# Rescheduling the first periods of a fused linear-attention and SwiGLU kernel, with q.kv in 64x64 tiles, one wide z broadcast and q transposed by DMA

## The chip, the cores and the metric

One Trainium2 chip (trn2), one core of it. The metric is the device time of one execution in microseconds, from runs without a profile, given as the median of several. The profile is one profiled execution; its span (first to last instruction) lies about 2 us below the run's time.

Engine names in the profile: PE is TensorE (matmuls), PEld its weight loads, DVE is VectorE, ACT is ScalarE, POOL is GpSimd, SP is SyncE (here it only issues DMAs).

## The reference, cut to what matters

```python
# q, k, v: 8 batches x 8 heads x 576 tokens x 64, float32
def _attn_ref(q, k, v):
    def phi(x): return np.where(x > 0, x, np.exp(x) - 1.0) + 1.0
    q_p, k_p = (phi(q), phi(k))
    kv = np.einsum('bhsd,bhse->bhde', k_p, v)        # one 64x64 matrix per head
    z = np.sum(k_p, axis=2)
    num = np.einsum('bhsd,bhde->bhse', q_p, kv)
    den = np.einsum('bhsd,bhd->bhs', q_p, z)[..., None] + 1e-06
    return (num / den)

def _moe_ref(x, w_gate, w_val, w_out):               # x: 4608 tokens x 512
    g = x @ w_gate                                   # 512 -> 1536
    silu = g * (1.0 / (1.0 + np.exp(-g)))
    return (silu * (x @ w_val)) @ w_out              # 1536 -> 512
```

## The kernel before

The network's 4608 tokens are done in nine *periods* of 512 tokens. A period g has twelve gate/value blocks (`l1`, eight 128x512 matmuls each) and four output blocks (`l2`, twelve matmuls each). A batch has nine slices j of 64 tokens, with one half of the heads (hh = 0) on partitions 0 to 63 and the other on 64 to 127; a period takes eight slices, so most periods take slices of two batches. While period g runs, the attention of batch g+1 is spread over its twelve `l1` slots and four `l2` slots, between the network's matmuls. In the traces each engine takes its calls in the order of the program (in run 7 below, ScalarE stands 7.33 us before one exp while a silu behind it has its input), so the slot of a call decides its place on each engine.

The attention steps that matter here:

```python
    def mm1(b, lp):              # kv and, in an extra column of ones, z
        if lp == 0:
            kvb[b] = (bank(), bank())
        W = 2 * D + 1
        for j in range(J):
            for hh in range(2):
                rows = slice(C * hh, C * hh + C)
                nc.tensor.matmul(
                    out=kvb[b][hh][:, 256 * lp:256 * lp + W], lhsT=kp[b % 2][rows, j, P * lp:P * lp + P],
                    rhs=vm[b % 2][rows, j, :, :].rearrange("p l c -> p (l c)")[:, 130 * lp:130 * lp + W],
                    start=(j == 0), stop=(j == J - 1))
    # zdiag (DVE): id16 * z column -> zd;  r_copies (ACT): kv blocks -> R
    def zb(b):                   # z broadcast over the partitions
        zps[b] = (bank(),) * 2
        for hh in range(2):
            nc.tensor.matmul(out=zps[b][hh][C * hh:C * hh + C, 0:HL * D], lhsT=ones[:, 0:C],
                             rhs=zd[:, 2 * hh:2 * hh + 2, :].rearrange("p i c -> p (i c)"), start=True, stop=True)
    # s3_prod, s3_reduce, s3_recip, s3_scale (DVE): q := q / (q.z), three groups of three slices (c = 0, 1, 2)
    def tr(b, c):                # transposes of q on TensorE, then tr_copy on ACT into qT
        ...
                nc.tensor.transpose(out=pt[:, 2 * jj + lp, :], in_=qp[b % 2][:, j0 + jj, P * lp:P * lp + P],
                                    identity=id16[:, :])
    def mm2(g, i, eng):          # q.kv -> xT[i], the network's input; R is block-diagonal 128x128
        ps = bank()
        ...
            nc.tensor.matmul(out=ps[:, c0:c0 + C * len(js)], lhsT=R[b % 2][:, i, :],
                             rhs=qT[b % 2][:, i, js[0]:js[-1] + 1, :].rearrange("p j c -> p (j c)"),
                             start=True, stop=True)
        # eviction to xT[i] by ACT or DVE
```

The schedules of before: `early` (periods 0 and 1: exp, phi, direct z sums `z_direct`, scaling and mm1 all inside the period before use; silu of four blocks by tanh, so that it shares a table with exp: in the trace no table load, 1.28 us each, stands between them), `late` (period 2) and `steady` (periods 3 to 6). The start of the program and the loads:

```python
    load(k, k16, 0, 0, 2)
    ...
    ld_v(0)
    ld_w1(0)
    ld_k(1)
    ld_w1(1)
    ld_w1(2)
    ld_q(1)
    ...
    def steady(b):
        sl[0] = [lambda: phi_q(b, 0), lambda: mm1(b, 0)]
        sl[1] = [lambda: phi_q(b, 1), lambda: mm1(b, 1)]
        sl[2] = [lambda: zdiag(b, 0), lambda: zdiag(b, 1), lambda: r_copies(b)]
        sl[3] = [lambda: zb(b), lambda: zb_copy(b), lambda: s3_prod(b, 0)]
        ...
        w = [
            [lambda: s3_scale(b, 2)],
            [lambda: tr(b, 2), lambda: tr_copy(b, 2, A)],
            [lambda: mm2(b, 0, V), lambda: mm2(b, 1, A)],
            [lambda: mm2(b, 2, V), lambda: mm2(b, 3, A)],
        ]
```

Of the kernel before, what the change touches and what calls it, by code (L numbers as in the profile page):

```python
# [17 lines left out]
def kernel(  # L18
# [47 lines left out]
    R = two([P, 4, P], FP16, "R")  # L66
    qT = two([P, 4, J, C], FP16, "qT")
# [20 lines left out]
    def chan(i):  # L88
        return 2 * (i % 2) + i // 2
# [30 lines left out]
    def phi(src, e, dst, b, lp):  # L120
        s = slice(2 * lp, 2 * lp + 2)
        nc.vector.tensor_scalar(out=e[:, s, :], in0=e[:, s, :], scalar1=1.0, scalar2=None, op0=ALU.min)
        for l in range(2 * lp, 2 * lp + 2):
            nc.vector.scalar_tensor_tensor(  # L124
                out=dst[b % 2][:, :, D * l:D * l + D],
                in0=src[b % 2][:, l, :].rearrange("p (j d) -> p j d", d=D), scalar=0.0,
                in1=e[:, l, :].rearrange("p (j d) -> p j d", d=D), op0=ALU.max, op1=ALU.add)
# [14 lines left out]
    def vcast(b, lp):  # L142
        s = slice(2 * lp, 2 * lp + 2)
        nc.scalar.activation(out=vm[b % 2][:, :, s, 0:D].rearrange("p j l d -> p l j d"),
                             in_=v16[b % 2][:, s, :].rearrange("p l (j d) -> p l j d", d=D),
                             func=AF.Copy, bias=0.0, scale=1.0)
# [4 lines left out]
    def mm1(b, lp):  # L151
        if lp == 0:
            kvb[b] = (bank(), bank())
        W = 2 * D + 1
        for j in range(J):
            for hh in range(2):
                rows = slice(C * hh, C * hh + C)
                nc.tensor.matmul(
                    out=kvb[b][hh][:, 256 * lp:256 * lp + W], lhsT=kp[b % 2][rows, j, P * lp:P * lp + P],
                    rhs=vm[b % 2][rows, j, :, :].rearrange("p l c -> p (l c)")[:, 130 * lp:130 * lp + W],  # L160
                    start=(j == 0), stop=(j == J - 1))
# [7 lines left out]
    def r_copies(b):  # L169
        for hh in range(2):  # L170
            kvv = kvb[b][hh][:, :].rearrange("p (i c) -> p i c", i=2)
            for h2 in range(2):
                rows, c = slice(D * h2, D * h2 + D), (D + 1) * h2
                nc.scalar.activation(
                    out=R[b % 2][rows, :, D * h2:D * h2 + D].rearrange("p (l a) c -> p a l c", a=2)[:, hh, :, :],
# [5 lines left out]
    def zb(b):  # L181
        zps[b] = (bank(),) * 2
        for hh in range(2):
            nc.tensor.matmul(out=zps[b][hh][C * hh:C * hh + C, 0:HL * D], lhsT=ones[:, 0:C],
                             rhs=zd[:, 2 * hh:2 * hh + 2, :].rearrange("p i c -> p (i c)"), start=True, stop=True)

    def zb_copy(b):
        nc.scalar.activation(out=zbc[:, :], in_=zps[b][0][:, 0:HL * D], func=AF.Copy, bias=0.0, scale=1.0)
# [43 lines left out]
    def tr(b, c):  # L232
        j0, j1 = js_of(c)
        tps[(b, c)] = bank()
# [6 lines left out]
    def tr_copy(b, c, eng):  # L241
        j0, j1 = js_of(c)
        src = tps[(b, c)][:, :].bitcast(FP16)[:, 0:2 * P * (j1 - j0)].rearrange("p (j i c) -> p j i c", j=j1 - j0, i=4)
        dst = qT[b % 2][:, :, j0:j1, :].rearrange("p i j c -> p j i c")
# [9 lines left out]
    def mm2(g, i, eng):  # L254
        ps = bank()
        us = units(g)
        for b in sorted(set(u[0] for u in us)):
            js = [j for (bb, j) in us if bb == b]
            c0 = C * us.index((b, js[0]))
            nc.tensor.matmul(out=ps[:, c0:c0 + C * len(js)], lhsT=R[b % 2][:, i, :],  # L260
                             rhs=qT[b % 2][:, i, js[0]:js[-1] + 1, :].rearrange("p j c -> p (j c)"),
                             start=True, stop=True)
        dst = xT[i][g % 2][:, :]
        if eng == "A":
            nc.scalar.activation(out=dst, in_=ps[:, :], func=AF.Copy, bias=0.0, scale=1.0 / SC)
        else:
            nc.vector.tensor_scalar(out=dst, in0=ps[:, :], scalar1=1.0 / SC, scalar2=None, op0=ALU.mult)  # L267


    def l1(g, fb, tanh=False):  # L270
        pg, pv = pG[fb % 2], pV[fb % 3]
        for (w, ps) in ((wg, pg), (wv, pv)):
            for i in range(4):
                nc.tensor.matmul(out=ps[:, :], lhsT=w[:, chan(i), P * fb:P * fb + P], rhs=xT[i][g % 2][:, :],  # L274
# [34 lines left out]

    load(k, k16, 0, 0, 2)  # L310
    load(k, k16, 0, 2, HL)
    load(q, q16, 0, 0, 2)
    nc.gpsimd.iota(out=idx[:, :], pattern=[[-1, P]], base=0, channel_multiplier=1)
# [3 lines left out]
    ld_k(1)  # L317
    ld_w1(1)
    ld_w1(2)
    ld_q(1)  # L320
# [5 lines left out]
    nc.vector.memset(ones[:, :], 1.0)  # L326
    nc.vector.memset(sil[0][:, :], 0.0)
    for i in range(2):
        nc.vector.memset(vm[i][:, :, :, D:D + 1], 1.0)
        nc.vector.memset(R[i][:, :, :], 0.0)  # L330

    A, V = "A", "V"

# [5 lines left out]
    def s3_all(b, c):  # L339
        s3_prod(b, c)  # L340
        s3_reduce(b, c)
        s3_recip(b, c)
        s3_scale(b, c)

# [3 lines left out]
    nc.vector.tensor_scalar(out=id16[:, :], in0=idx[:, :], scalar1=0.0, scalar2=None, op0=ALU.is_equal)  # L348
# [4 lines left out]
    for lp in range(2):  # L353
        vcast(0, lp)
        mm1(0, lp)
    r_copies(0)
    for c in ((0, 3), (3, 6), (6, 8)):
        s3_all(0, c)
        if c[0] == 6:
            warm(6)  # L360
        tr(0, c)
        tr_copy(0, c, A)
    warm(2)
    for i in range(4):
        mm2(0, i, A if i % 2 else V)
    warm(2)

    def s3a(b, c):
        return [lambda: s3_prod(b, c), lambda: s3_reduce(b, c)]

    def early(b):

        sl = [[] for _ in range(FB)]
        sl[0] = [lambda: exp_k(b, 0)]
        if b == 1:
            c8 = (8, 9)
            sl[5] = [lambda: s3_all(0, c8), lambda: tr(0, c8), lambda: tr_copy(0, c8, A)]
        sl[1] = [lambda: exp_k(b, 1)]
        sl[2] = [lambda: exp_q(b, 0)]
        sl[3] = [lambda: exp_q(b, 1)]  # L380
        sl[4] = [lambda: phi_k(b, 0)]
        sl[6] = [lambda: phi_k(b, 1)]
        sl[7] = [lambda: z_direct(b)]
        sl[8] = [lambda: phi_q(b, 0)]
        sl[10] = [lambda: phi_q(b, 1)]
        sl[11] = s3a(b, 0)
        w = [
            [lambda: s3_recip(b, 0), lambda: s3_scale(b, 0)] + s3a(b, 1)
            + [lambda: s3_recip(b, 1), lambda: tr(b, 0), lambda: tr_copy(b, 0, A)],
            [lambda: vcast(b, 0), lambda: vcast(b, 1), lambda: s3_scale(b, 1)] + s3a(b, 2)  # L390
            + [lambda: tr(b, 1), lambda: tr_copy(b, 1, A), lambda: s3_recip(b, 2), lambda: s3_scale(b, 2)],
            [lambda: mm1(b, 0), lambda: mm1(b, 1), lambda: r_copies(b), lambda: tr(b, 2), lambda: tr_copy(b, 2, A)],
            [lambda i=i: mm2(b, i, A if i % 2 else V) for i in range(4)],
        ]
        return sl, w

    def steady(b):

        sl = [[] for _ in range(FB)]
        sl[0] = [lambda: phi_q(b, 0), lambda: mm1(b, 0)]  # L400
        sl[1] = [lambda: phi_q(b, 1), lambda: mm1(b, 1)]
        sl[2] = [lambda: zdiag(b, 0), lambda: zdiag(b, 1), lambda: r_copies(b)]
        sl[3] = [lambda: zb(b), lambda: zb_copy(b), lambda: s3_prod(b, 0)]
        sl[4] = [lambda: s3_reduce(b, 0)]
        sl[5] = [lambda: s3_recip(b, 0), lambda: s3_prod(b, 1)]
        sl[6] = [lambda: s3_scale(b, 0)]
        sl[7] = [lambda: s3_reduce(b, 1), lambda: tr(b, 0), lambda: tr_copy(b, 0, A)]
        sl[8] = [lambda: s3_recip(b, 1), lambda: s3_prod(b, 2)]
        sl[9] = [lambda: s3_scale(b, 1)]
        sl[10] = [lambda: s3_reduce(b, 2), lambda: tr(b, 1), lambda: tr_copy(b, 1, A)]  # L410
        sl[11] = [lambda: s3_recip(b, 2)]
        w = [
            [lambda: s3_scale(b, 2)],
            [lambda: tr(b, 2), lambda: tr_copy(b, 2, A)],
            [lambda: mm2(b, 0, V), lambda: mm2(b, 1, A)],
            [lambda: mm2(b, 2, V), lambda: mm2(b, 3, A)],
        ]
        return sl, w

    def late(b):  # L420

        sl = [[] for _ in range(FB)]
        sl[0] = [lambda: phi_k(b, 0)]
        sl[1] = [lambda: phi_k(b, 1), lambda: mm1(b, 0)]
        sl[2] = [lambda: phi_q(b, 0), lambda: mm1(b, 1)]
        sl[3] = [lambda: zdiag(b, 0), lambda: zdiag(b, 1), lambda: r_copies(b)]
        sl[4] = [lambda: phi_q(b, 1), lambda: zb(b), lambda: zb_copy(b)]
        sl[5] = [lambda: s3_prod(b, 0)]
        sl[6] = [lambda: s3_reduce(b, 0)]
        sl[7] = [lambda: s3_recip(b, 0), lambda: s3_prod(b, 1)]  # L430
        sl[8] = [lambda: s3_scale(b, 0)]
        sl[9] = [lambda: s3_reduce(b, 1), lambda: tr(b, 0), lambda: tr_copy(b, 0, A)]
        sl[10] = [lambda: s3_recip(b, 1), lambda: s3_prod(b, 2)]
        sl[11] = [lambda: s3_scale(b, 1)]
        w = [
            [lambda: s3_reduce(b, 2), lambda: s3_recip(b, 2), lambda: tr(b, 1), lambda: tr_copy(b, 1, A)],
            [lambda: s3_scale(b, 2)],
            [lambda: tr(b, 2), lambda: tr_copy(b, 2, A), lambda: mm2(b, 0, V)],
            [lambda: mm2(b, 1, V), lambda: mm2(b, 2, A), lambda: mm2(b, 3, V)],
        ]  # L440
        return sl, w

# [70 lines left out]
```

## Time and profile before

368.75 us, median of 3 runs (368.16 to 369.24). From the page of the profile:

```profile
span 366.4 us, 4976 instructions
...
PE 326.5 (89%) x1866; PEld 153.9 (42%) x1866; DVE 231.4 (63%) x408; ACT 180.8 (49%) x266; POOL 39.3 (11%) x66
```

TensorE is the engine to look at. A busy share of 89% says little by itself: 1296 network matmuls start 0.2158 us apart when nothing hinders them, 31.08 us a period (144 x 0.2158), 279.7 us in nine. So I cut the span at the first gate matmul of each period. In the view by stretches (`--windows`), each line is a stretch (from:to), its length, then for PE, PEld, DVE, ACT and POOL the busy time and number of instructions, the granted TensorE clock, the DMA share and GB/s:

```profile
...
27.60:76.18 48.58, 37.85 (x228) 17.75 (x227) 29.75 (x52) 20.77 (x32) 8.55 (x14) 0.96 0.97 163
76.18:118.86 42.68, 38.05 (x225) 18.20 (x224) 29.17 (x49) 29.30 (x39) 3.65 (x6) 0.96 0.35 59
...
227.09:262.70 35.61, 35.41 (x211) 16.45 (x210) 26.52 (x48) 21.56 (x31) 0.00 (x0) 1.00 0.13 31
...
```

These are periods 0 and 1 and one of the four steady periods (3 to 6, all 35.6). Period 0 lasts 17.5 us longer than its matmuls, period 1 11.6, a steady one 4.5. What TensorE waited for, in all (line, matmul output, what it waited for, total us, times, longest):

```profile
...
PE pX_112 L238 <- DVE qp_73 L226: 7.6, 3, 5.0
PE pX_114 L238 <- DVE qp_73 L226: 2.4, 2, 1.9
PE pG_108 L274 <- DVE sil_97 L279: 2.3, 1, 2.3
```

(Left out above them: the wait for the first load, in the start.) The 5.0 us is in period 0: the transposes of the ninth slice wait for VectorE, which waited for ScalarE, which waited for the load of batch 1's q (ScalarE's timeline; the bracket is the idle time before, and what ended it):

```profile
36.24 1.16 ACT L118 ACTIVATE eq<-q_1_66 128x1152 f16<-128x1152 f16 x1 [3.52 <-DMA q_1_66<-in_q_dram]
```

Waits of that kind are most of the early periods' loss; matmuls at half rate after them are another part (six start 0.43 us apart from 45.8 to 47.9 us, right after the 5.0 us). In a steady period there is nearly none; there the 4.5 us is attention work on TensorE. Part of one, from the timeline (start, length with the pipeline's drain, line, output<-inputs, count):

```profile
220.70 0.50 PE L238 MATMUL pX_112<-id_105,qp_74 128*128 128x128 f16 x6
221.03 2.75 PE L293 MATMUL pV_110<-wo,hT_94 128*128 128x512 f16 x12
223.62 0.30 PE L260 MATMUL pX_113<-qT_84,R_82 128*128 128x320 f16 x1
...
224.06 2.75 PE L293 MATMUL pG_108<-wo,hT_94 128*128 128x512 f16 x12
227.31 0.38 PE L274 MATMUL pG_107<-xT_1_89,wg 128*128 128x512 f16 x1
227.89 0.38 PE L274 MATMUL pG_107<-xT_1_91,wg 128*128 128x512 f16 x1 [0.20 <-DVE xT_1_91 L267]
```

Lengths overlap, so read the distance between starts: a transpose block takes 221.03 - 220.70 = 0.33 us, mm2 two times 0.44, and the third gate matmul comes 0.58 instead of 0.22 us after the second, as xT (the network's input) is not yet there.

### The profile page before, as it was taken

Reading aid. Unit: us, or ns where it says so; the run is one execution under the profiler, and the core shown is the slowest. Engines: PE = TensorE matmul, PEld = TensorE weight load, DVE = VectorE, ACT = ScalarE, POOL = GpSimd, SP = SyncE. Lnnn points to the kernel's source line nnn. Section 1 sums busy time; section 2 is a strip of 40 time slices with the busy share of each in tenths; the row PEclk is TensorE's granted clock in tenths of the full one; section 3 lists DMA queues with packets and bytes.
Section 4 is the critical chain, followed back from the end, with each engine's and each line's share of the span. In section 5 each row is a group of like instructions: output and inputs, shape, how many; then the busy total and the mean of one; then the engine's idle time right before and its main releaser. Section 6 shows DMA issues by size and latency. Waiting matters only on the chain.

```text
span 366.4 us, 4976 instructions
## 1 busy us (share of the span) xinstructions
PE 326.5 (89%) x1866; PEld 153.9 (42%) x1866; DVE 231.4 (63%) x408; ACT 180.8 (49%) x266; POOL 39.3 (11%) x66
## 2 busy tenths in 40 slices
PE   0469288999879899999999999999999999999995
PEld 0334043543435344544454444444444444444442
DVE  2974639747595788787767885788488533323331
ACT  3645531576576348545854585459544234402310
POOL 8532211100111120111011000000000000000000
PEclk9999989999899999999999999999999999999999
DMA  7999994830446257348054703100300130022013
GB/s 107 196 206 207 207 187 64 144 90 2 64 64 126 58 73 121 71 110 131 0 87 98 126 2 86 29 2 18 82 18 2 29 87 2 0 57 59 0 29 86
DMA packets 23656, 28.63 MB, mean 78 GB/s; under 512 B 2128, under 2 KB 19024, under 8 KB 23632
## 3 DMA queue, kind: packets, MB, share of 16 engines
q0 software_dynamic: 17872, 18.88, 33.0%
q1 hardware_dynamic: 5760, 9.44, 10.3%
q8 instruction: 14, 0.23, 0.3%
q14 instruction: 10, 0.08, 0.1%
HBM read 37.75 MB, written 9.44 MB: 129 GB/s over the span
## 4 chain that ended last, share of the span: by engine, by line
PE 70%; DVE 12%; DMA 7%; issue 5%; ACT 3%; POOL 2%; DVEq 0%; POOLq 0%; ACTq 0%
PE pG_107 L274 11%; PE pG_108 L274 9%; PE pV_109 L274 7%; PE pV_111 L274 7%; PE pV_110 L274 6%; PE pG_108 L293 6%; PE pV_110 L293 6%; PE pG_107 L293 5%; PE pV_109 L293 5%; DMA q_1_66<-in_q_dram 4%; DMA wv<-in_moe_w_val_dram 3%; DVE hT_94 L283 2%; DVE den L213 1%; PE pX_112 L238 1%; DVE qp_74 L124 1%
## 5 line engine op out<-in xcount | busy, mean ns | idle before, releaser
L274 PEld LDWEIGHTS <-wv 128*128 128x128 f16 x432 | 42.5, 98 | 52.5 <-issue 2.6
L274 PEld LDWEIGHTS <-wg 128*128 128x128 f16 x432 | 40.6, 98 | 51.3 <-issue 8.1
L282 ACT ACTIVATE sil_96<-pG_107 128x512 f16<-128x512 f32 x50 | 29.9, 597 | 38.8 <-PE pG_107 L274 36.5
L282 ACT ACTIVATE sil_97<-pG_108 128x512 f16<-128x512 f32 x50 | 29.8, 597 | 36.3 <-PE pG_108 L274 33.0
L293 PEld LDWEIGHTS <-hT_94 128*128 128x128 f16 x240 | 23.2, 98 | 26.3
L293 PEld LDWEIGHTS <-hT_95 128*128 128x128 f16 x192 | 18.6, 98 | 21.1
L213 DVE TENSOR_REDUCE den<-prod 128x12 f32<-128x768 f16 (+2 forms) x25 | 22.9, 915 | 0.3
L195 PE MATMUL pX_113<-kp_71,ones 64*64 64x256 f16 x18 | 4.0, 402 | 11.6 <-DVE kp_71 L124 11.6
L293 PE MATMUL pV_110<-wo,hT_94 128*128 128x512 f16 x60 | 13.8, 379 | 0.0
L293 PE MATMUL pG_108<-wo,hT_94 128*128 128x512 f16 x60 | 13.8, 379 | 0.0
L293 PE MATMUL pV_109<-wo,hT_94 128*128 128x512 f16 x60 | 13.8, 379 | 0.0
L293 PE MATMUL pG_107<-wo,hT_94 128*128 128x512 f16 x60 | 13.8, 379 | 0.0
L283 DVE SCALAR_TENSOR_TENSOR hT_94<-pV_109,sil_96 128x512 f16<-128x512 f32 x10 | 6.9, 691 | 10.6 <-PE pV_109 L274 5.8
L274 PE MATMUL pG_108<-xT_0_86,wg 128*128 128x512 f16 x30 | 11.4, 380 | 2.3 <-DVE sil_97 L279 2.3
L274 PE MATMUL pG_107<-xT_0_90,wg 128*128 128x512 f16 x30 | 11.6, 387 | 0.4 <-DVE xT_0_90 L267 0.4
L226 DVE TENSOR_TENSOR qp_73<-qp_73,rden 128x768 f16<-128x768 f16 (+2 forms) x13 | 11.6, 892 | 0.3
L274 PE MATMUL pG_107<-xT_0_86,wg 128*128 128x512 f16 x30 | 11.7, 390 | 0.0
L274 PE MATMUL pG_107<-xT_0_92,wg 128*128 128x512 f16 x30 | 11.6, 387 | 0.0
L274 PE MATMUL pG_107<-xT_0_88,wg 128*128 128x512 f16 x30 | 11.6, 387 | 0.0
L118 ACT ACT_TABLE_LOAD x7 | 9.0, 1283 | 5.3 <-DMA k_0_63<-in_k_dram 5.2
L124 DVE SCALAR_TENSOR_TENSOR kp_72<-k_1_64,ek 128x576 f16<-128x576 f16 x16 | 11.4, 755 | 0.3
L124 DVE SCALAR_TENSOR_TENSOR kp_71<-k_0_63,ek 128x576 f16<-128x576 f16 x16 | 11.4, 755 | 0.3
(188 smaller groups left out, 751.9 us busy)
## 6 DMA issues: line engine op xcount, KB each, us to landing
out_dram<-osb_98 SPq DMA_DIRECT2D x24, 128.0 KB, 2.4
out_dram<-osb_99 SPq DMA_DIRECT2D x24, 128.0 KB, 2.4
out_dram<-osb_100 SPq DMA_DIRECT2D x24, 128.0 KB, 2.4
v_0_67<-in_v_dram POOLq DMA_DIRECT2D x8, 288.0 KB, 6.7
k_1_64<-in_k_dram POOLq DMA_DIRECT2D x8, 288.0 KB, 5.2
q_1_66<-in_q_dram POOLq DMA_DIRECT2D x8, 288.0 KB, 5.0
v_1_68<-in_v_dram POOLq DMA_DIRECT2D x8, 288.0 KB, 6.6
k_0_63<-in_k_dram POOLq DMA_DIRECT2D x6, 288.0 KB, 4.8
```

The lines of the kernel that those rows point to most:

```text
L118: nc.scalar.activation(out=e[:, s, :], in_=src[b % 2][:, s, :], func=AF.Exp, bias=0.0, scale=1.0)
L124: nc.vector.scalar_tensor_tensor(out=dst[b % 2][:, :, D * l:D * l + D], in0=src[b % 2][:, l, :].rearrange("p (j d) -> p j d", d=D), scalar ...
L195: nc.tensor.matmul(out=zps[b][hh][rows, 0:HL * D], lhsT=ones[rows, 0:C], rhs=kp[b % 2][rows, j, :], start=(j == 0), stop=(j == J - 1))
L213: nc.vector.tensor_reduce(out=den[:, HL * j0:HL * j1], in_=prod[:, 0:j1 - j0, :].rearrange("p j (l d) -> p (j l) d", d=D), axis=AX.X, op=A ...
L226: nc.vector.tensor_tensor(out=qv, in0=qv, in1=rden[:, HL * j0:HL * j1].unsqueeze(2).to_broadcast([P, HL * (j1 - j0), D]), op=ALU.mult)
L238: nc.tensor.transpose(out=pt[:, 2 * jj + lp, :], in_=qp[b % 2][:, j0 + jj, P * lp:P * lp + P], identity=id16[:, :])
L274: nc.tensor.matmul(out=ps[:, :], lhsT=w[:, chan(i), P * fb:P * fb + P], rhs=xT[i][g % 2][:, :], start=(i == 0), stop=(i == 3))
L282: nc.scalar.activation(out=s[:, :], in_=pg[:, :], func=AF.Silu, bias=0.0, scale=1.0)
L283: nc.vector.scalar_tensor_tensor(out=hT[g % 2][:, fb, :], in0=pv[:, :], scalar=SC * (0.5 if tanh else 1.0), in1=s[:, :], op0=ALU.mult, op1 ...
L293: nc.tensor.matmul(out=ps[:, :], lhsT=hT[g % 2][:, fb, P * t:P * t + P], rhs=wo[:, fb, :], start=(fb == 0), stop=(fb == FB - 1))
```

## The change

Its intent: take attention work off TensorE in the steady periods, and reorder the first two so that fewer engines wait. (a) mm2 becomes one pass of 64x64 tiles, four at a time, over the kv blocks themselves instead of block-diagonal 128x128 matrices, half of which are zeros, and moves ahead of the last output block (from period 1 on), so that its evictions are hidden. The heads are reordered for that. (b) z is broadcast by one full matmul of 512 columns. (c) mm1 is one block. (d) From batch 3 on q is transposed by DMA. (e) Loads, exps and the schedules of the first periods move: batch 1's q loads ahead of the second and third weight blocks, the loads of later batches and the exps of batches 1 and 2 come earlier, tanh stays in two blocks of period 0 only, and period 1 takes the `late` form, period 2 the steady one.

The diff, cut to its core:

```diff
-    R = two([P, 4, P], FP16, "R")
-    qT = two([P, 4, J, C], FP16, "qT")
+    R = two([P, 4, D], FP16, "R")
+    qT = two([P, J, 2, P], FP16, "qT")
 ...
-        zps[b] = (bank(),) * 2
+        zps[b] = bank()
+        nc.tensor.matmul(out=zps[b][:, :], lhsT=ones[:, :], rhs=zd[:, :, :].rearrange("p i c -> p (i c)"),
+                         start=True, stop=True)
 ...
     def tr(b, c):
         j0, j1 = js_of(c)
+        if b > 2:
+            nc.sync.dma_start_transpose(out=qT[b % 2][:, j0:j1, :, :].rearrange("p j l t -> p (j l) t"),
+                                        in_=qp[b % 2][:, j0:j1, :].rearrange("p j c -> p (j c)"))
+            return
 ...
+    def mm2(g, spare, engs):
+        ps = [bank(), bank(), bank(), spare]
+        ...
+                for lp in range(2):
+                    for e in range(2):
+                        rows = slice(D * e, D * e + D)
+                        nc.tensor.matmul(out=ps[2 * hh + e][D * lp:D * lp + D, c0:c0 + C * len(js)],
+                                         lhsT=R[b % 2][rows, 2 * lp + hh, :],
+                                         rhs=qT[b % 2][rows, js[0]:js[-1] + 1, lp, C * hh:C * hh + C],
+                                         start=True, stop=True)
 ...
     ld_k(1)
+    ld_q(1)
     ld_w1(1)
     ld_w1(2)
-    ld_q(1)
 ...
+        if c[0] == 3:                      # in the start-up
+            exp_k(1, 0)
+            exp_k(1, 1)
 ...
+    def first():                           # period 0; (slot, call)
+            (0, lambda: exp_q(1, 0)), (1, lambda: exp_q(1, 1)),
+            (2, lambda: phi_k(1, 0)), (4, lambda: phi_k(1, 1)), (5, lambda: z_direct(1)),
+            (6, lambda: phi_q(1, 0)), (7, lambda: phi_q(1, 1)),
+            (8, lambda: s3_a(0, c8)), (9, lambda: s3_b(0, c8)), (10, lambda: t_(0, c8)),
+            (10, lambda: s3_a(1, 0)), (11, lambda: s3_b(1, 0))])
+        ...                                # output blocks
+            (0, lambda: vcast(1, 0)), (0, lambda: vcast(1, 1)), (0, lambda: s3_a(1, 1)), (0, lambda: s3_b(1, 1)),
+            (1, lambda: t_(1, 0)), (1, lambda: s3_a(1, 2)), (1, lambda: exp_k(2, 0)), (1, lambda: exp_k(2, 1)),
+            (2, lambda: t_(1, 1)), (2, lambda: mm1(1)), (2, lambda: r_copies(1)), (2, lambda: s3_b(1, 2)),
+            (2, lambda: exp_q(2, 0)), (2, lambda: exp_q(2, 1)),
+            (3, lambda: t_(1, 2))])
 ...
-            l1(g, fb, tanh=(g < 2 and fb < NT))
+            l1(g, fb, tanh=(g == 0 and fb < 2))
 ...
         for t in range(4):
+            if t == 3 and b1 < NG and g > 0:
+                mm2(b1, pV[2], "AVAV")
             l2(g, t)
```

## The prediction

> **What bounds it now.** TensorE. In the timeline, back-to-back 128x512 matmuls start every 0.2158 us, so one period of the gated network (144 matmuls) costs 31.08 us, nine of them 279.7 of the 366.4 us span. The stretches between the periods' first gate matmuls: start-up 27.6, period 0 48.6, period 1 42.7, period 2 37.2, periods 3 to 6 35.4 to 35.6, period 7 32.5, period 8 31.1, tail 4.5 us. Granted clock 0.96 to 1.00. Start-up is 8% of the span; periods 0 and 1 exceed pure matmul time by 29 us, another 8%.
>
> Period 0's excess is mostly waits (list of waits): 5.0 us for the scaled ninth q slice, 2.3 us for a tanh fix behind a late q load, 1.9 and 1.0 for scale and phi. Period 1: 2.0, 1.9, 1.5.
>
> **A steady period's 4.5 us of attention on TensorE (timeline):** three transpose blocks 3 x 0.33; mm1 in two blocks 2 x 0.71, about 0.2 of each for changing the array's tiling (the Trainium skill, "TensorEngine Tiling (Array Packing)", Key Properties, says a mode change drains the array; the trace's longer spacing around the block agrees); z broadcast 0.49; mm2 0.88 plus 0.2 to 0.4 waiting for xT.
>
> **The change there.** DMA transposes take 1.0 off TensorE. One mm1 block saves 0.2. One z matmul of 512 columns saves 0.27. Four 64x64 tiles: estimate 2 x 0.22 + 0.2 for 0.88, and the xT evictions hide under the last output block: 0.5 together. The trace shows 64x64 tiles concurrent only in pairs (256 columns every 0.107 us); the same page, Available Configurations, lists four independent ones, which no run here shows. Sum about 2.1: 33.4 us. I stepped VectorE through it (26.5 us of work): it keeps up, zdiag just in time for the z matmul.
>
> The transposes' latency is off the path: a slice is scaled 6 us or more before the mm2 that reads it, the third a period before.
>
> **Early periods.** Period 0: q of batch 1 loads before the later weight blocks, exp of k moves ahead, tanh shrinks from four blocks to two. VectorE stays nearly full (about 31 us). Stepped through: waits of 2 us at z, 1.4 at the ninth slice, then at the end a serial chain (ScalarE's exp and copies, transpose, copy, mm2, xT) with 4 us of idle TensorE: 42.3 us. Period 1 takes period 2's form minus the savings: 36.2. Period 2 becomes steady: 33.5. Start-up: the exp table load (1.28 us) moves off, but loads bind again and exp of k1 delays the last q copy: gain 0.3. Period 7: gain 0.7.
>
> **Sum of gains, all on the TensorE path:** 0.3 + 6.3 + 6.5 + 3.7 + 4 x 2.1 + 0.7 = 26: span 340.5; runs lie about 2 us above it: 342.5 us. Range 337 to 349. Faster by over 2%: 0.97; within 2%: 0.02; slower: 0.01.
>
> **What would show each step.** Steady periods of 33.2 to 33.7 us; mm2 under 0.7 us; one mm1 block of 1.2 us; period 0 between 39 and 44 us with its largest TensorE wait at its end; period 1 about 36; first gate matmul near 27.3 us.
>
> **What would make it wrong.** (1) mm2's tiles do not overlap, or weight loads bind: up to 1.2 us a period, 9 in all. (2) DMA transposes slower than 6 us: TensorE waits before mm2 in periods 2 and 3. (3) VectorE's lag in early periods: plus or minus 4 us. (4) TensorE at half clock after waits (spacing 0.43 us, as at 45.8 us before): 1 to 3 us. (5) Reordered loads delay weight blocks past their use.

## The result, and the profile after

341.06 us, median of 4 runs (339.46 to 341.98), against 368.46 us for before (4 runs); ratio 0.926, 95% interval 0.921 to 0.931. Ratios here are the mean time of one kernel's fast runs over that of the other's fast runs of the same rounds, so not quite the ratio of the medians quoted. The prediction was 342.5 us, 337 to 349.

The page after:

```profile
span 340.2 us, 4865 instructions
...
PE 310.7 (91%) x1814; PEld 145.3 (43%) x1814; DVE 228.5 (67%) x405; ACT 170.1 (50%) x256; POOL 39.1 (11%) x66
```

The stretches after, cut the same way (periods 0 and 1 and one steady period):

```profile
...
27.19:69.85 42.66, 37.47 (x234) 17.94 (x234) 28.74 (x51) 24.15 (x36) 7.93 (x13) 0.96 1.10 194
69.85:106.01 36.16, 34.71 (x216) 16.45 (x216) 30.28 (x55) 25.65 (x36) 4.90 (x8) 1.00 0.42 71
...
205.97:239.30 33.33, 33.33 (x199) 15.33 (x198) 26.58 (x48) 19.48 (x29) 0.00 (x0) 1.00 0.28 54
...
```

In the steady period TensorE now counts as busy for all of its 33.33 us (a matmul's length includes its drain, so gaps of 0.1 us, like the one before the z broadcast below, do not show). All stretches, with what was predicted for each:

| stretch | before, us | predicted gain | measured after, us | measured gain |
|---|---|---|---|---|
| start | 27.60 | 0.3 | 27.19 | 0.4 |
| period 0 | 48.58 | 6.3 | 42.66 | 5.9 |
| period 1 | 42.68 | 6.5 | 36.16 | 6.5 |
| period 2 | 37.01 | 3.7 | 33.32 | 3.7 |
| periods 3 to 6, each | 35.61 | 2.1 | 33.32 | 2.3 |
| period 7 | 32.31 | 0.7 | 31.74 | 0.6 |
| period 8 and tail | 35.79 | 0 | 35.84 | -0.05 |

The gain of the start is not resolved: in the runs below that leave its order alone it ends between 26.5 and 27.7 us.

The waits of TensorE after:

```profile
...
PE pX_113 L273 <- ACT qT_85 L254: 2.5, 1, 2.5
...
PE pX_114 L197 <- DVE kp_72 L124: 1.5, 1, 1.5
PE pX_112 L183 <- DVE zd L165: 0.9, 1, 0.9
```

The waits of 5.0 and 2.3 us are gone. The three longest of what is left lie in periods 0 and 1 (those left out here are in the start): 2.5 us at the end of period 0 (mm2 waits for ScalarE's copy of the transposed q), 1.5 us at the direct z sums in period 0, 0.9 us at the z broadcast in period 1.

And a steady period's mm2, where the timeline of before showed its own:

```profile
202.81 0.32 PE L273 MATMUL pX_113<-qT_84,R_82 64*64 64x320 f16 x1
...
202.82 0.32 PE L273 MATMUL pX_114<-qT_84,R_82 64*64 64x320 f16 x1
202.97 0.24 PE L273 MATMUL pX_113<-qT_85,R_83 64*64 64x192 f16 x1
...
203.37 2.76 PE L308 MATMUL pG_108<-wo,hT_94 128*128 128x512 f16 x12
```

Four tiles (one is left out) start within 0.01 us, the next four 0.16 us later (320 columns). The whole pass, from where the next output matmul would have started (200.13 + 12 x 0.2158 = 202.72) to 203.37, takes 0.65 us against 0.88, and the gate matmuls wait for nothing. The Trainium skill, "TensorEngine Tiling (Array Packing)", Available Configurations, lists 64x64 as four tiles; the trace agrees: all four run at once.

### The profile page after: what moved, and what is told of

Its sections match the earlier page's. It is cut to its first block, busy times and chain, and to the rows that moved or that the text cites. A ratio compares the mean times of both kernels' runs of the same rounds, so it can differ in the third digit from the quotient of the medians.

```text
span 340.2 us, 4865 instructions
## 1 busy us (share of the span) xinstructions
PE 310.7 (91%) x1814; PEld 145.3 (43%) x1814; DVE 228.5 (67%) x405; ACT 170.1 (50%) x256; POOL 39.1 (11%) x66
## 4 chain that ended last, share of the span: by engine, by line
PE 75%; DMA 14%; ACT 3%; DVE 3%; issue 2%; POOL 2%; POOLq 0%; DVEq 0%
PE pG_108 L289 12%; PE pG_107 L289 12%; PE pV_111 L289 8%; PE pV_110 L289 8%; PE pV_109 L289 8%; DMA q_1_66<-in_q_dram 7%; PE pG_108 L308 6%; PE pV_110 L308 6%; PE pG_107 L308 6%; PE pV_109 L308 6%; DMA v_1_68<-in_v_dram 6%; PE pX_113 L158 2%; DMA k_0_63<-in_k_dram 2%; PE pX_113 L273 1%; ACT eq L118 1%
## 5 line engine op out<-in xcount | busy, mean ns | idle before, releaser
L289 PEld LDWEIGHTS <-wg 128*128 128x128 f16 x432 | 41.7, 98 | 53.5 <-issue 5.7
L297 ACT ACTIVATE sil_96<-pG_107 128x512 f16<-128x512 f32 x53 | 31.6, 597 | 56.3 <-PE pG_107 L289 54.8
L297 ACT ACTIVATE sil_97<-pG_108 128x512 f16<-128x512 f32 x53 | 31.6, 597 | 38.8 <-PE pG_108 L289 36.7
L197 PE MATMUL pX_113<-kp_71,ones 64*64 64x256 f16 x9 | 2.1, 409 | 11.8 <-DVE kp_71 L124 11.8
L298 DVE SCALAR_TENSOR_TENSOR hT_94<-pV_109,sil_96 128x512 f16<-128x512 f32 x10 | 6.9, 688 | 8.4 <-PE pV_109 L289 8.4
L298 DVE SCALAR_TENSOR_TENSOR hT_94<-pV_109,sil_97 128x512 f16<-128x512 f32 x10 | 6.9, 690 | 7.9 <-ACT sil_97 L297 5.0
L289 PE MATMUL pG_107<-xT_0_86,wg 128*128 128x512 f16 x30 | 11.6, 387 | 0.4 <-DVE xT_0_86 L282 0.4
L289 PE MATMUL pG_107<-xT_0_92,wg 128*128 128x512 f16 x30 | 11.6, 388 | 0.0
L289 PE MATMUL pG_107<-xT_0_90,wg 128*128 128x512 f16 x30 | 11.6, 387 | 0.0
L289 PE MATMUL pG_107<-xT_0_88,wg 128*128 128x512 f16 x30 | 11.6, 387 | 0.0
L124 DVE SCALAR_TENSOR_TENSOR qp_74<-q_1_66,eq 128x576 f16<-128x576 f16 x16 | 11.4, 755 | 0.3
```

What stands on the lines that cost most here:

```text
L124: nc.vector.scalar_tensor_tensor(out=dst[b % 2][:, :, D * slot(l):D * slot(l) + D], in0=src[b % 2][:, l, :].rearrange("p (j d) -> p j d", ...
L197: nc.tensor.matmul(out=zps[b][hh][rows, 0:HL * D], lhsT=ones[rows, 0:C], rhs=kp[b % 2][rows, j, :], start=(j == 0), stop=(j == J - 1))
L289: nc.tensor.matmul(out=ps[:, :], lhsT=w[:, i, P * fb:P * fb + P], rhs=xT[i][g % 2][:, :], start=(i == 0), stop=(i == 3))
L297: nc.scalar.activation(out=s[:, :], in_=pg[:, :], func=AF.Silu, bias=0.0, scale=1.0)
L298: nc.vector.scalar_tensor_tensor(out=hT[g % 2][:, fb, :], in0=pv[:, :], scalar=SC * (0.5 if tanh else 1.0), in1=s[:, :], op0=ALU.mult, op1 ...
```

## The experiments

Twelve runs, all correct; each is an edit of the kernel after, except where said. The period lengths come from each run's profile, cut at the first gate matmul, and repeat to 0.04 us in steady periods (one of 33.68 in run 8 aside), so they resolve differences that the times (spread about 1 us) do not. One caution for all: the profiled run of after happens to have a slow start, with TensorE at half rate in its first eight matmuls, about 1.6 us lost (see below). Period 0 of after's form was 42.66 there, 42.6 in run 1, which starts at half rate too, and 41.2 to 41.9 in runs 2 to 6, which do not (one matmul of run 6 aside). Period 1 varies likewise: 36.2 in after and 36.9 in run 5, where its first eight matmuls ran at half rate.

### 1. Transposes on TensorE again (pe_transposes)

```diff
-        if b > 2:
+        if b > 99:
```

> After, with the DMA transposes undone: all batches transposed on TensorE and copied out by ScalarE. My theory: each of the periods 2 to 6 gets back its three blocks of 0.33 us on TensorE and nothing else changes, so steady periods go from 33.32 to 34.3 us and the time rises by 5.0 us. Rival A: what counts is ScalarE, freed of three 0.8 us copies; then TensorE waits for ScalarE appear and the steady period goes beyond 34.6. Rival B: the transposes hold up the output writes in SyncE's queue, so that undoing them costs less than 3 us.

Measured: 348.16 us (ratio to before 0.947), 7.1 us above after's 341.06. Steady periods 34.66 to 34.70, plus 1.36. My theory of 1.0 is off, and rival B falls. Rival A named the mark of 34.6, but not for its reason: no steady-state wait for ScalarE is in the list. The size is in the timeline: each block of transposes between gate blocks takes longer than the one between output blocks.

```profile
224.18 1.03 PE L289 MATMUL pV<-xT,wv 128*128 128x512 f16 x4
225.20 0.51 PE L244 MATMUL pX<-id,qp 128*128 128x128 f16 x6
```

The four value matmuls from 224.18 would let the next one start at 225.04 (4 x 0.2158). The transposes start at 225.20. Their weight loads (q itself is the stationary operand) had to wait:

```profile
225.20 0.34 PEld L244 LDWEIGHTS <-qp 128*128 128x128 f16 x6 [0.49 <-DVE qp L228]
```

VectorE finished scaling the slice at 225.15. Two blocks of 0.51 us and one of 0.33 give 1.35. (In before the block between gate blocks takes 0.50 us as well, from 243.22 to 243.72.) So a DMA transpose saves the block and also the wait for its input. The list of waits of TensorE's matmuls did not show it; the row of the weight loads did.

### 2. mm2 behind the last output block (mm2_after_last_block)

```diff
-            if t == 3 and b1 < NG and g > 0:
-                mm2(b1, pV[2], "AVAV")
             l2(g, t)
+            if t == 3 and b1 < NG and g > 0:
+                mm2(b1, pV[2], "AVAV")
```

> After, with mm2 of periods 1 to 7 moved behind the last output block, where before had it; still one pass of 64x64 tiles. Theory of the prediction: what the earlier place hides is a wait of 0.2 to 0.4 us for xT, so 7 x 0.3 = 2 us in all. Rival, from the end of period 0 after the change, where mm2 still stands there: the first gate matmul starts about 0.8 us after mm2's last matmul, against 0.2 us for the next matmul otherwise, because all four evictions now come after one short pass; then each of seven periods grows by 0.6 to 0.7 us, 4 to 5 us in all.

Measured: 346.09 us (ratio 0.943), plus 5.0; steady periods 34.23, plus 0.91, more than either expected. The timeline shows two parts. The first gate matmul comes 1.20 us after the last output block instead of mm2's 0.65: plus 0.55, with a wait of 0.47 for xT.

```profile
207.59 1.10 PE L289 MATMUL pG<-xT,wg 128*128 128x512 f16 x4 [0.47 <-ACT xT L280]
...
216.24 0.38 PE L183 MATMUL pX<-zd,ones 128*128 128x512 f16 x1 [0.26 <-DVE zd L165]
```

The rest, 0.38, is up to the z broadcast: it starts 8.65 us after the period's first gate matmul, 8.27 in after; 0.08 of it is a slower first gate block, 0.30 a longer wait for zdiag. ScalarE now loads its silu table only when the evictions are done, after the period has begun:

```profile
208.04 1.28 ACT L297 ACT_TABLE_LOAD   x1
```

VectorE stands for it:

```profile
209.97 0.69 DVE L298 SCALAR_TENSOR_TENSOR hT<-pV,sil 128x512 f16<-128x512 f32 x1 [1.11 <-ACT sil L297]
```

So the first silu, the first product on VectorE, and all that VectorE does in order after it (phi of q, then zdiag) start late, and TensorE meets that delay at the z broadcast. In after the table load ends at 172.33 (171.05 + 1.28), before the period begins at 172.65. This chain is read from the traces; no run moved the table load alone. In before, too, it came after the period's start (227.90 against 227.09).

### 3. mm2 on the full array (mm2_full_array)

```diff
-    R = two([P, 4, D], FP16, "R")
+    R = two([P, 4, P], FP16, "R")          # block-diagonal again, heads in the order of before
 ...
-                        nc.tensor.matmul(out=ps[2 * hh + e][D * lp:D * lp + D, c0:c0 + C * len(js)],
-                                         lhsT=R[b % 2][rows, 2 * lp + hh, :], ...
+                nc.tensor.matmul(out=ps[i][:, c0:c0 + C * len(js)], lhsT=R[b % 2][:, i, :], ...
```

> After, with mm2 in one pass at the new place, but with full-array matmuls over block-diagonal weights (heads, v and weight blocks ordered as before). Theory: the four tiles do run at once; undoing them makes mm2 0.88 us plus nothing for the tiling change, instead of 0.65: steady periods 33.5 to 33.6, and plus 1.5 to 2.0 us over eight passes. Rival: four 64x64 tiles gain nothing over the full array because loads and the tiling change eat it: period within 0.05 us of 33.32.

Measured: 341.96 us (ratio 0.931). Steady periods 33.52 to 33.53, plus 0.20, as the theory said; the rival falls. The time rose by 0.9 us, under the 1.5 to 2.0 expected; the medians' spread is of that size, and eight passes at 0.2 would make 1.6.

### 4. z broadcast in two halves (zb_two_halves)

```diff
-        zps[b] = bank()
-        nc.tensor.matmul(out=zps[b][:, :], lhsT=ones[:, :], rhs=zd[:, :, :]...
+        zps[b] = (bank(),) * 2
+        for hh in range(2):
+            nc.tensor.matmul(out=zps[b][hh][C * hh:C * hh + C, 0:HL * D], lhsT=ones[:, 0:C], ...
```

> After, with the z broadcast again as two matmuls of 64 output rows and 256 columns, and one copy. Theory: the change of tiling before and after costs 0.2 us or more, the block goes from 0.33 (of which 0.11 is a wait) to 0.45-0.5 us: plus 0.1 to 0.2 us a period, six times, about 1 us in all. Rival: the z matmul waits for VectorE's zd anyway, so the broadcast's own length is hidden: 0.

Measured: 340.78 us (ratio 0.928), steady periods 33.32, the same as after to the last digit. The rival's number is right, its reason only in part. The block before the broadcast ends at 179.99 here; the halves start when zdiag is done and the next gate matmul follows 0.24 us later:

```profile
180.08 0.30 PE L184 MATMUL pX<-zd,ones 128*64 128x256 f16 x2
180.32 1.04 PE L287 MATMUL pG<-xT,wg 128*128 128x512 f16 x4
```

The two halves use different columns of the array and run at the same time: the second starts 0.03 us after the first (at 180.12), and 256 columns take 0.107. So from the first half to the next gate matmul there are 0.24 us, 0.10 of them for going back from 128x64 tiles; the wide matmul takes 0.22. Going to the tiles falls within the wait for zdiag, and that is all that is hidden. Hence two halves cost about as much as the one wide matmul. The 0.49 us that I read off the trace before (from the end of the block at 235.81 to 236.30) held two waits for zdiag, 0.12 and 0.13, as the second half stood there for the last piece of zd:

```profile
235.93 0.43 PE L184 MATMUL pX_113<-zd,ones 128*64 128x256 f16 x2
236.30 0.39 PE L274 MATMUL pG_107<-xT_1_87,wg 128*128 128x512 f16 x1
```

In after this stretch is 0.34 us. As run 4 shows, the gain is not the wide matmul's; zdiag is less late. The silu table, which is loaded before the period now (run 2), fits as the reason, but was not tested alone.

### 5. mm1 in two blocks (mm1_two_blocks)

```diff
-            (0, lambda: phi_q(b, 0)), (1, lambda: phi_q(b, 1)), (1, lambda: mm1(b)),
+            (0, lambda: phi_q(b, 0)), (0, lambda: mm1(b, (0,))), (1, lambda: phi_q(b, 1)), (1, lambda: mm1(b, (1,))),
```

> After, with mm1 of the five steady periods again in two blocks (after the first and after the second gate block). Theory of the prediction: one more change of tiling costs 0.2 us a period, so steady periods 33.52 and plus 1.0 us. Rival, formed after zb_two_halves cost nothing: TensorE waits for zd before the z broadcast in every steady period (0.11 us in the trace), so the first 0.11 us of the loss is absorbed there and the period is 33.4 (plus 0.5 us in all), or is hidden altogether.

Measured: 341.56 us (ratio 0.931), steady periods 33.41, plus 0.09. The rival is right: TensorE arrives at the z broadcast later and no longer waits there. The cost of the second block itself is 0.21 us, but 0.12 of it is paid out of the wait for zdiag:

```profile
213.15 1.03 PE L290 MATMUL pV<-xT,wv 128*128 128x512 f16 x4
214.01 0.38 PE L184 MATMUL pX<-zd,ones 128*128 128x512 f16 x1
```

(213.15 + 4 x 0.2158 = 214.01: no wait is left.)

### 6. All steady parts undone (early_reschedule_alone)

The four edits above together with mm2 in two halves at the places of before; the start and periods 0 to 2 keep their new order.

> After, with all four steady-state parts undone at once: TensorE transposes, full-array mm2 in two halves at the old places (also for period 8's input), z broadcast in halves, mm1 in two blocks in the steady periods. What is left of the change is the rescheduling of periods 0 to 2 and of the start. Theory: steady periods return to the 35.6 us of before, periods 0 and 1 keep most of their gain (about 43 and 37.5), period 2 is 35.6: time 354 to 356, about half of the whole gain. Rival: the four parts overlap so much (their single effects add up to 1.36 + 0.91 + 0.20 + 0 + mm1, over 2.5 us, against the 2.29 us that a steady period gained) that together they give back under 2.0 us a period, time under 352.

Measured: 352.53 us (ratio 0.962). Steady periods 35.60 to 35.62: exactly before's length. Periods 0, 1 and 2 are 41.85, 36.05 and 35.60. The theory's period lengths hold, the rival's do not; the time came in 1.5 us below the theory's range since periods 0 and 1 were shorter than I allowed. The single effects of runs 1 to 5 add up to 1.36 + 0.91 + 0.20 + 0 + 0.09 = 2.56 us against 2.29 together: they overlap. Mm2 in two halves at the old place exposes 0.37 us of wait for xT after the second gate matmul in this run's trace, where the single pass of run 2 exposes 0.55 before the first. In time, the reschedule alone is worth 366.72 - 352.53 = 14.2 us and the steady parts on top of it 352.53 - 341.06 = 11.5 us (the medians are of different rounds, so good to about 1 us).

### 7. Batch 1's q loaded late (q1_loaded_late)

```diff
     ld_k(1)
-    ld_q(1)
     ld_w1(1)
     ld_w1(2)
+    ld_q(1)
```

> After, with the load of batch 1's q put back behind the second and third weight blocks. Theory: period 0's new order lives on that load: exp of q stands in ScalarE's order right after the first two tanh, so q landing near 36 us instead of 24 to 28 stops ScalarE, then the gate banks, and period 0 grows by 4 to 7 us. Rival: the wait moves into slack that VectorE's 31 us of work leaves anyway (z waits for phi at 40 us), and the time rises by less than 2 us.

Measured: 348.62 us (ratio 0.950), plus 7.6; period 0 takes 48.40 us, as long as before's 48.58; period 1 grew too, to 37.46, with its first eight matmuls at half rate. Without the early load nothing of period 0's gain is left in the new order; whether that load alone would give it in the old order was not run. ScalarE stands 7.33 us before exp of q (from this run's timeline):

```profile
35.94 1.16 ACT L118 ACTIVATE eq<-q 128x1152 f16<-128x1152 f16 x1 [7.33 <-DMA q<-in_q_dram]
```

And the longest wait of TensorE in the same run, from the list of waits:

```profile
PE pG L289 <- DVE sil L294: 6.1, 1, 6.1
```

The expectation was 4 to 7 us for period 0. It is not slack that was moved; the rival falls.

### 8. exp of k of batch 1 inside period 0 (exp_k1_in_period_0)

```diff
-        if c[0] == 3:
-            exp_k(1, 0)
-            exp_k(1, 1)
 ...
-            (0, lambda: exp_q(1, 0)), (1, lambda: exp_q(1, 1)),
+            (0, lambda: exp_k(1, 0)), (1, lambda: exp_k(1, 1)), (2, lambda: exp_q(1, 0)), (3, lambda: exp_q(1, 1)),
 ...
-            l1(g, fb, tanh=(g == 0 and fb < 2))
+            l1(g, fb, tanh=(g == 0 and fb < 4))
```

> After, with exp of k of batch 1 moved from the start-up back into period 0's first two blocks, exp of q into the third and fourth, and tanh in four blocks as before; loads as after. Theory: VectorE gets two more 0.69 us fixes and phi of k starts no later, as exp of k at 29 us still comes before its phi at 36 us, so period 0 grows by 1 to 2 us at most. Rival: the early exp is a main part of period 0's gain, and it grows by 3 us or more.

Measured: 341.51 us (ratio 0.932), period 0 41.68 us, against 41.2 to 41.4 in runs 2, 4 and 5, which start at full rate as this one does: a rise of 0.3 to 0.5 us, and none in the time that the spread lets one see. The rival falls, and so does most of my 1 to 2 us. The early exp of k and the smaller number of tanh blocks are not where the gain is.

### 9. Periods 1 and 2 in their old order (periods_1_2_old_order)

```diff
-        elif g == 1:
+        elif g == 1:
+            sl, w = old1(b1)      # the early form of before, without its exps and tanh; mm2 behind the last block
+        elif g == 2:
             sl, w = late(b1)
```

> After, with periods 1 and 2 in the order that before gave them (phi of k, z by direct sums and all scaling inside period 1, mm1 in its last blocks and mm2 behind it; period 2 in the late form), but without their exps, which period 0 does already, and without tanh. Theory: period 1's gain of 6.5 us is the order: z from mm1 and scaling spread over the gate blocks, so the old order brings back waits for kp and qp and a serial end: period 1 at 40 us or more, period 2 about 34.5 to 35, time plus 5 us or more. Rival: the gain is the work that left the period (four tanh fixes of 0.69 us on VectorE, four exps and two table loads on ScalarE), so the old order without them costs little: period 1 under 38 us.

Measured: 347.26 us (ratio 0.944), plus 6.2; period 1 takes 40.92 and period 2 35.35. The theory holds: the order (with mm2's place in it) is most of period 1's gain, not the exps and tanh fixes that left it: 4.8 of 6.5 us against after. In this profile, though, the first eight matmuls of period 1 ran at half rate; against run 5, where they did so too (36.92), the order is worth 4.0 of 5.8 us. Within period 1 the waits for kp (1.0 us, at the direct z sums) and for the scaled q (1.9 us) are back:

```profile
PE pX L244 <- DVE qp L228: 2.1, 2, 1.9
PE pX L197 <- DVE kp L124: 1.0, 1, 1.0
```

(This is the list for period 1 alone, 67.9 to 109 us.)

### 10. The early waits reordered away (early_waits_removed)

The profile after names the waits that are left in periods 0 and 1, so this run takes them away by order alone:

```diff
-            (4, lambda: phi_k(1, 1)), (5, lambda: z_direct(1)),
+            (4, lambda: phi_k(1, 1)), (6, lambda: z_direct(1)),
-            (9, lambda: s3_b(0, c8)), (10, lambda: t_(0, c8)),
+            (9, lambda: s3_b(0, c8)), (11, lambda: t_(0, c8)),
-            (0, vcast(1, .)), (0, s3_a(1, 1)), (0, s3_b(1, 1)), (1, t_(1, 0)), (1, s3_a(1, 2)), (1, exp_k(2, .)),
-            (2, t_(1, 1)), (2, mm1(1)), (2, r_copies(1)), (2, s3_b(1, 2)), (2, exp_q(2, .)), (3, t_(1, 2))
+            (0, vcast(1, .)), (0, exp_k(2, .)), (0, mm1(1)), (0, r_copies(1)), (0, t_(1, 0)), (0, s3_a(1, 1)), (0, s3_b(1, 1)),
+            (1, t_(1, 1)), (1, s3_a(1, 2)), (1, s3_b(1, 2)), (2, exp_q(2, .)), (2, t_(1, 2))
-            late: (4, zb(b)), (4, zb_copy(b))
+            late: (5, zb(b)), (5, zb_copy(b))
```

Besides, iota and the identity matrix made from it move behind the first k and q loads, and six warming matmuls are added in the start (the text says eight instead of four more; it is four after the first transposes and six in place of four later).

> After, with the waits that its trace shows in periods 0 and 1 reordered away: exp of k of batch 2, mm1 and its copies one output block earlier, exp of q and the last transposes before the last output block of period 0, the z sums of batch 1 and the ninth slice's transposes one block later, the z broadcast of batch 2 one block later; iota after the first loads; eight instead of four warming matmuls more in the start. Theory: at its end period 0 waits for ScalarE (2.5 + 0.5 us for qT and xT), and for VectorE at z (1.5) and the ninth slice (0.8); taking these away gives 4 to 5 us there and 0.9 us in period 1: 335 to 337 us. Rival: VectorE, busy nearly all of period 0, is the real limit and the waits only move: within 1.5 us of 341.

Measured: 334.10 us (ratio 0.909), 7 us below after and better than expected; start 26.50, period 0 37.54 (half rate at its start, as in after), period 1 35.24. The waits for z and for the ninth slice in period 0 and for zdiag in period 1 are gone from the list. What is left of TensorE's waits from period 0 on is 0.6 us twice and 0.5 us. VectorE was not the limit; the rival falls.

### 11. The same, with DMA transposes from batch 1 on (early_waits_and_dma_from_1)

```diff
-        if b > 2:
+        if b > 0:
```

> The same, with q transposed by DMA from batch 1 on instead of batch 3. Theory: TensorE loses six more blocks of 0.33 to 0.49 us in periods 0 and 1 and ScalarE six copies of 0.8 us; the last slice of batch 1 needs about 3 us by DMA (2.7 measured after) while one output block of 2.6 us runs, so a wait of up to 1 us may come: 1.5 to 2.5 us faster than the same without. Rival: in period 0 the loads of weights, k, q and v share the DMA engines and the transposes land late (over 4 us), so that period 0 grows and the gain is under 0.5 us.

Measured: 340.74 us (ratio 0.927), 6.6 us slower than run 10. Period 0 grew from 37.54 to 43.42. The rival is right about the cause: mm2 at the end of period 0 waits for a transpose.

```profile
PE pX L273 <- DMA qT<-qp: 6.4, 1, 6.4
```

For the transposes of period 0 alone, the view of the DMA issues gives from issue to landing:

```profile
DMA to landing us min/median/max: 8.3/9.6/10.0
```

And for those of the whole run:

```profile
DMA to landing us min/median/max: 2.7/2.8/10.0
```

The stretch in question, 50 to 70 us, has the DMA engines full (share 1.12, 205 GB/s), with k, q and v of batch 3 still loading:

```profile
50.00:70.00 20.00, 13.29 (x102) 6.34 (x101) 10.88 (x20) 10.82 (x16) 1.42 (x3) 0.92 1.12 205
```

So the price is that of starting in period 0, beside the loads, not of DMA transposes as such. The Trainium skill, "DMA: Bandwidth & Descriptors", Issuing engines are not separate DMA queues, says that DMAs of different issuing engines run on the same 16 engines and interleave; the trace agrees: these transposes come from SyncE, the loads from GpSimd, and beside them a landing takes 9.6 us instead of 2.8.

### 12. The same, from batch 2 on, with more warming (early_waits_dma_from_2)

```diff
-        if b > 2:
+        if b > 1:
 ...
-            warm(6)
+            warm(8)
 ...
-    warm(2)
+    warm(5)
     mm2(0, pV[2], "VAVA")
+    warm(3)
```

> As early_waits_removed, but q transposed by DMA from batch 2 on, and more warming matmuls before and after the first mm2, in time that TensorE idles. Theory, from the two runs before: the DMA transposes fail in period 0 only, where the loads keep the DMA engines full (9.6 us to landing against 2.8); in period 1 they land in about 3 us and take 1.0 to 1.3 us off it: 34.1 us. The first gate blocks run at 0.43 us a matmul for about 1.7 us of loss, and the warming takes 1 to 1.5 us of that away: 331 to 332.5 us in all. Rival: the clock at the start depends on more than the last microseconds, the first blocks stay at 0.43 us, and only the 1 us of period 1 comes: 333 us.

Measured: 332.45 us, median of 6 runs (331.96 to 333.33), ratio to before 0.904, 95% interval 0.902 to 0.906. This is the best version: its ratio is 0.976 of after's (0.9041 / 0.9259). Period 1 takes 33.48 us (expected 34.1), nearly a steady one; the transposes land in 5.6 us at most. It also differs in the clock of its profiled run, from the timeline of the first gate and value blocks (x4, four matmuls):

```profile
26.68 1.19 PE L289 MATMUL pG<-xT,wg 128*128 128x512 f16 x4
27.70 1.02 PE L289 MATMUL pV<-xT,wv 128*128 128x512 f16 x4
```

The next block starts at 28.57, so a block of four takes 1.02 and 0.87 us here. In the profiled run of after the same blocks start at 27.19, 28.85 and 30.56: 1.66 and 1.71, about half rate. It would be easy to credit the added warming, but the profiles speak against so simple a reading: run 10, which has more warming than after too, starts at half rate (26.50, 28.16, 29.84), and run 9, which has none added, starts fast (26.80, 27.83, 28.69), as do runs 2 to 5, 7 and 8. Whether the warming of run 12 helps stays open. Six runs of this version spread over 1.4 us, four of after over 2.5.

## Why the prediction was right

The time (341.06 against 342.5) and the span (340.2 against 340.5) are right, and so is every stretch within 0.4 us. Parts of that are luck, as the steps show:

- **What bounds the kernel: right.** Gains appeared where TensorE's work or waits went, and edits that touched only other engines' work (run 8) moved nothing.
- **Transposes off TensorE, "1.0": right mechanism, term too small.** 1.36 us a period (run 1). I measured the block between output blocks and took the two between gate blocks to be equal; those carried a wait of 0.16 us for VectorE's scaling each.
- **One mm1 block, "0.2": right for the block, too large for the period.** The block shrank from 2 x 0.71 to 1.22 us, but the period by 0.09 (run 5), since TensorE spends the rest waiting for zdiag.
- **z broadcast, "0.27": wrong.** 0.00 (run 4). I booked waits for VectorE, half of the 0.49 us, as work of TensorE, and missed that the two halves run at the same time. The step that failed is reading 0.49 us between two starts as the block's length without looking at what ended just before.
- **mm2 "0.5 together": right as a sum with the old split, wrong in its parts.** The tiles alone give 0.20 (run 3), as 0.88 against 0.65. The place is worth 0.91 for a single pass (run 2), 0.55 of it for xT and the rest up to the z broadcast, by the trace because of the late silu table load. Before had split mm2, with 0.36 us of wait for xT.
- **The sum of these, "about 2.1": 2.29 measured.** The errors have opposite signs (transposes +0.36, z -0.27), so part of the precision is luck.
- **VectorE "keeps up, zdiag just in time": right, and it mattered more than I said.** It is the reason for the zero in run 4 and the 0.09 in run 5.
- **Period 0, "42.3": 42.66 in the profile,** but with other parts: waits of 1.5 at z (2 said), 0.8 at the ninth slice (1.4 said), 2.9 at its end (4 said), and in this run about 1.6 us of half rate at its start, which I had named only as a risk. So this match is luck too: without that, the same period took 41.2 to 41.4 us (runs 2, 4, 5). That the gain needs the early load of q is shown by run 7.
- **Period 1 "36.2" and period 2 "33.5": 36.16 and 33.32.** That order more than the lighter load did period 1 is shown by run 9. (A slip in the prediction: the 1.5 us that it lists last under period 1's waits lies in period 2, at 124.2 us.)
- **Transpose latency off the path: right** for batches 3 and on, 2.7 to 3.4 us to landing. It would have been wrong for batch 1 (run 11).

## What to carry to other kernels

When one engine is the bottleneck, cut the span into its periods and predict each from distances between instruction starts; but look at what ended just before a short block, as a wait for another engine looks like work until the block is made shorter and nothing happens. The place of evictions and table loads around a period's first instruction can cost more than the arithmetic that is saved (0.91 against 0.20 us here). A transfer moved from an engine to DMA is free only where the DMA engines are: the same transposes took 2.7 us in a quiet period and up to 10 us beside the loads of period 0, and putting one load back in the queue cost 7.6 us.

## What the Trainium skill lacked or had wrong

- "TensorEngine Tiling (Array Packing)", Key Properties: it says that changing the tiling mode drains the array, and gives no figure for it. Here it is about 0.09 us each way for changes that split the rows (mm2: last output matmul's successor due at 202.72, first tile at 202.81; last tiles end their stream at about 203.28, next matmul at 203.37), and about 0.10 us back from 128x64 (run 4: second half at 180.12, 0.107 for its columns, next matmul at 180.32).
- "TensorEngine Tiling (Array Packing)", Available Configurations: no page has a measurement of four 64x64 tiles at once. Here they start within 0.01 us, and the next four 0.13 to 0.16 us later for 320 columns; one full-array matmul of that length in before takes 0.14.
- "DMA: Bandwidth & Descriptors", Rules for kernel authors: it says that a transpose next to ordinary DMAs needs nothing. The row is about corrupted data, and all results here were correct, so the data agree; what it lacks is the time: an SBUF to SBUF transpose of 128x768 fp16 landed in 2.7 to 3.4 us in the quiet periods of after and in 8.3 to 10.0 us beside GpSimd-issued loads that filled the engines (205 GB/s, run 11). The page gives a bandwidth for DMA transposes, no landing time.
- "TensorE: Matmul & The Clock Gate", Why this matters for your kernels: it advises against idle gaps over about 3 us, and elsewhere says that frequent short idles can slow the clock too, without a length. In after's profiled run TensorE was at full rate at 22.04 us (four warming matmuls 0.22 us apart) and at half rate from 24.6 us (two warming matmuls 0.43 us apart) to 30.56; the one gap between them is 1.15 us, before 24.2. So half rate can come after a gap well under 3 us; the runs do not show the rule.
